# Tile 2 of x loaded on ScalarE's queue instead of SyncE's

## The chip, the cores and the metric

The kernel runs on one core of a Trainium2 chip. The metric is the device time of one execution in microseconds (us). A core has five engines with instruction streams of their own: TensorE (PE in the profile, with its weight loads PEld), VectorE (DVE), ScalarE (ACT), GpSimd (POOL) and SyncE (SP). SP, ACT and POOL also start DMA transfers; these run on the core's 16 DMA engines. A DMA started by SP stands in the profile's queue q1, one started by ACT in q10, one started by POOL in q0.

## The reference

The inputs are x (2048 tokens by 640), the attention weights wqkv (640 by 1920) and wo (640 by 640), and the weights w1 (640 by 1728) and w2 (1728 by 640) of a dense block, all in bf16. x is normalised over its 640 columns. One branch is linear attention with 32 heads of width 20, the other a two-layer block with a ReLU; the output is x + s * silu(g).

```python
xn  = layernorm(x)
q, k, v = split(xn @ wqkv)                # 32 heads, width 20
phi = lambda t: where(t > 0, t + 1, exp(t)) + 1e-6
kv  = einsum("bhsd,bhse->bhde", phi(k), v);  z = sum_s phi(k)
s   = (phi(q) @ kv / (phi(q) @ z + 1e-6)) @ wo
g   = relu(xn @ w1) @ w2
out = x + s * silu(g)
```

## The kernel before

The tokens are cut into 16 tiles of 128 rows (tile t is rows 128t to 128t+127 of x). The columns are cut into 5 chunks of 128, called k = 0 to 4, over which the products with wqkv and w1 accumulate in PSUM.

The whole kernel is a list of short words, `PROGRAM`. Each word records some operations with the tiles that they read and write. A planner (`Sched.place`, line 187) then gives every operation a time by fixed costs and puts the operations of each engine in order. PE and SP keep the order in which the words recorded them. So do all engines for the words ahead of the sign `|`; these words are called the head here. Behind the `|`, ACT, DVE and POOL take what is ready, by due time. `Sched.emit` then writes out each engine's stream with the semaphore waits. Every DMA has a semaphore of its own, and an engine that needs the data waits for it.

The planner has a model of the loads: all transfers share one line, each takes its bytes divided by a rate, and two fixed lags are added when the line passes two marks:

```python
lags = [(4.1, 0.6), (18.2, 1.2)]
...
line = max(est + (2.0 if c.turn else 1.5), line + (turned != c.turn) * (0.4 if c.turn else 0.8)) + c.byt
if lags and line > lags[0][0]:
    line += lags.pop(0)[1]
```

The words of the head that matter here:

- `lx2` loads tile 2 of x (160 KB) with SP, `ax1` loads tile 1 with ACT; both are `x_load` (line 560, the DMA at line 562).
- `lk02`, `lk24`, `lk45` load the key weights (the middle third of wqkv) in pieces of chunks 0-1, 2-3 and 4 with SP (`wk_load`, the DMA at line 586).
- `lw2`, `lw5`, `lw3`, `lw0` load pieces of w1 with SP (line 582).
- `ba0`, `bb0`, `ba3` are statistics of a tile's first or second half on DVE (`bn`, line 637). `ma0` to `ma3` are means on ACT (`mean_act`, line 685): of tiles 1 and 2 whole, of tiles 0 and 3 the second half. `sq1`, `sq2` are sums of squares on ACT (line 658).
- `ce0` to `ce3` subtract the mean on DVE (`centre`: line 699 for tiles 0 and 3, line 695 for tiles 1 and 2).
- `tr0` to `tr3` transpose a centred tile on PE (line 706), and `cd0`, `cd1`, `cd2` on DVE and `ca3` and on to `ca7` on ACT copy the transposed halves out of PSUM (lines 716 and 718): 0 and 1 are the two parts of tile 0, 2 and 3 those of tile 1, 4 and 5 those of tile 2, 6 and 7 those of tile 3.
- `k001`, `k012`, `k102` and so on are key products on PE (line 733): the first digit is the tile, the other two the range of chunks. The first two, `k001` and `k012`, need the first part of tile 0 (`cd0`) and the first key piece. `k023` is the first that needs the second piece.
- `S4`, `S5`, `S7`, `S6` are the full statistics of tiles 4 to 7 on DVE (line 637 twice and 641). `N1`, `N4`, `N5` and so on normalise a tile on DVE (line 673), and each is followed by a DMA transpose by SP (line 722), which brings the tile into the layout that the later products read. Tiles 0 to 3 thus exist twice: transposed on PE for the first key products, and transposed by DMA for what comes later.

On SP the order in the head is: loads of x tile 0, tile 2, key piece 0-1, x tile 3, key piece 2-3, x tiles 4 and 5, key piece 4, x tile 7, w1 piece 2, x tile 6, w1 pieces 5, 3 and 0, then the eight DMA transposes of tiles 1, 4, 5, 7, 6, 0, 2 and 3. ACT starts with a tiny activation (line 595), whose function table is loaded meanwhile, and the load of tile 1.

Behind the head most products use a Strassen scheme: of two tiles or blocks, sums and differences are made on DVE (line 936) and seven products on PE replace eight (line 1164 for blocks of 512 tokens, line 991 later on). The first of these sums, for the tokens 0 to 1023 (`T0`), need the DMA transposes of all the tiles 0 to 7.

Of the kernel before, what the change touches and what calls it, by code (L numbers as in the profile page):

```python
# [343 lines left out]


PROGRAM = """
lx0 lx2 ax1 ba0 mh0 ma0 lk02 lx3 lk24 ce0 lx4 ma1 ce1 lx5 lk45 lx7 lw2 tr0 pf3 cd0 lx6 bb0 ma2 sq1
ce2 cd1 ma3 tr1 k001 lw5 cd2 k012 ba3 lw3 ca3 mh3 ag0 ce3 S4 tr2 k102 S5 ca4 k023 k123 k134 ca5 k201
lw0 N1 tr3 N4 sq2 k213 S7 ca6 k035 ca7 k145 N5 ke0 k235 S6 bb3 N7 ag3 k301 k312 kr0 ke1 kr1 F1
N6 k325 ke2 P4 N0 kr2 P11 P5 F0 ke3 P10 KT5 kr3 KT4 N2 N3 |  # L350
# [1631 lines left out]
```

## Time and profile before

| what | value |
|---|---|
| median of 3 runs | 202.5 us (201.94 to 203.0) |
| profiled execution | 202.56 us |
| its span | 201.3 us |
| PE busy | 197.2 us |
| DVE busy | 173.2 us |
| ACT busy | 132.5 us |
| POOL busy | 37.7 us |
| share of the 16 DMA engines of q1, q0, q10 | 41.8%, 14.3%, 1.7% |
| granted clock of PE | 1.00 |

The span runs from the first to the last event that the profiler recorded; the execution's own time is 1.26 us longer. Rows of the timeline give the start in us from the span's start, the duration in us, the engine (with a q: its queue of DMA issues), the line, the operation, output and input, and how many instructions are merged. In brackets stands the idle time of the engine before it and what ended that. `reg` stands for several of the kernel's numbered buffers. In rows of the DMA view the last number is the median time from the start of the issue to the landing.

### The profile page before, as it was taken

To read this page: it belongs to the slowest core of one execution; us is meant where nothing else is said; L and a number is where in the kernel's file an instruction comes from. 1 tells how busy PE (TensorE), PEld (TensorE's weight loads), DVE (VectorE), ACT (ScalarE), POOL (GpSimd) and SP (SyncE) were. 2 spreads that over 40 slices of the span, in tenths; PEclk is the share of its full clock that TensorE was granted. 3 is DMA by queue.
4 is the path that set the end of the run, shared out by engine and by line. 5 is a ranking of instruction groups with operands and counts; after the bars stand their busy time and mean duration, and the time that the engine had idled before them with its cause. 6 is when DMAs were issued, how large, how long until landed. Compare 5 with 4: busy or idle time off the path is not lost.

```text
span 201.3 us, 3641 instructions
## 1 busy us (share of the span) xinstructions
PE 197.2 (98%) x1312; PEld 120.1 (60%) x1312; DVE 173.2 (86%) x407; ACT 132.5 (66%) x280; POOL 37.7 (19%) x66
## 2 busy tenths in 40 slices
PE   8899999999999999999999999999999999999995
PEld 2656534554564554545454777777777777777773
DVE  5998799999999989999568998999867699866565
ACT  6798958998999998868832514363545355536533
POOL 3584003143345646422000000000000000000000
PEclk9999999999999999999999999999999999999999
DMA  5999695345466798854304985975952711011113
GB/s 179 335 259 95 150 351 144 70 98 109 108 145 134 150 256 174 171 99 67 113 17 118 270 264 184 295 212 148 355 185 72 258 65 36 33 67 65 36 65 98
DMA packets 38455, 30.43 MB, mean 151 GB/s; under 512 B 13733, under 2 KB 38437, under 8 KB 38437
## 3 DMA queue, kind: packets, MB, share of 16 engines
q1 hardware_dynamic: 32853, 23.62, 41.8%
q0 software_dynamic: 4624, 5.57, 14.3%
q10 hardware_dynamic: 960, 1.02, 1.7%
q8 instruction: 10, 0.16, 0.4%
q14 instruction: 8, 0.07, 0.1%
HBM read 15.81 MB, written 5.24 MB: 105 GB/s over the span
## 4 chain that ended last, share of the span: by engine, by line
PE 90%; DVE 4%; DMA 2%; ACT 1%; issue 1%; DVEq 0%
PE psT L991 43%; PE psT L1164 32%; PE psT L733 6%; PE psT L1494 2%; PE psT L823 2%; DMA reg<-reg 1%; ACT regE L743 1%; PE psT L1838 1%; DMA reg<-in_A_x_dram 1%; PE psT L841 1%; PE psT L1629 1%; PE psT L1603 1%; DVE stats L637 1%; DVE regX L936 1%; PE psT L895 1%
## 5 line engine op out<-in xcount | busy, mean ns | idle before, releaser
L1164 PE MATMUL psT<-reg 128*128 128x512 bf16 (+2 forms) x166 | 45.0, 370 | 0.0
L991 PE MATMUL psT<-reg,regH 128*128 128x320 bf16 (+1 forms) x224 | 35.0, 299 | 0.0
L991 PE MATMUL psT<-reg 128*128 128x320 bf16 (+1 forms) x178 | 28.4, 299 | 0.0
L991 PEld LDWEIGHTS psT<-reg,regH 128*128 128x128 bf16 (+1 forms) x224 | 21.9, 98 | 8.5
L1164 PEld LDWEIGHTS psT<-reg 128*128 128x128 bf16 (+1 forms) x166 | 15.9, 98 | 16.9 <-DVE regH L1217 0.6
L863 POOL DMA_DIRECT2D regH<-reg x16 | 18.6, 1188 | 20.9 <-DMA regH<-reg 9.4
L991 PEld LDWEIGHTS psT<-reg 128*128 128x128 f16 (+1 forms) x178 | 17.3, 98 | 7.4 <-DVE regE L899 0.4
L936 DVE TENSOR_TENSOR reg<-reg 128x1024 f16<-128x1024 bf16 (+11 forms) x30 | 19.0, 646 | 2.2 <-PE psT L991 1.8
L998 ACT ACTIVATE reg<-psT 128x320 f32<-128x320 f32 (+1 forms) x24 | 10.5, 436 | 15.8 <-PE psT L991 14.8
L1214 ACT ACTIVATE regH<-psT 128x512 bf16<-128x512 f32 (+1 forms) x24 | 14.6, 612 | 5.8 <-PE psT L1164 5.3
L1665 ACT ACTIVATE wv_sb<-psT 128x320 bf16<-128x320 f32 (+2 forms) x23 | 9.6, 424 | 11.4 <-PE psT L991 11.0
L991 PE MATMUL psT<-reg,pqT 128*128 128x320 bf16 (+1 forms) x84 | 15.8, 299 | 0.0
L936 DVE TENSOR_TENSOR psT<-psT,reg 128x320 f32<-128x320 f32 (+1 forms) x21 | 11.4, 543 | 2.8 <-PE psT L991 2.8
L637 DVE BATCH_NORM_STATS2 stats<-reg 128x6 f32<-128x320 bf16 x28 | 12.3, 480 | 1.4 <-DMA reg<-in_A_x_dram 1.1
L1853 ACT ACTIVATE reg<-psT 128x640 bf16<-128x640 f32 (+1 forms) x14 | 8.0, 570 | 7.5 <-PE psT L991 7.5
L733 PE MATMUL psT<-reg 128*128 128x320 bf16 x80 | 12.3, 299 | 0.0
L936 DVE TENSOR_TENSOR reg<-psT,reg 128x320 bf16<-128x320 f32 (+1 forms) x16 | 7.8, 489 | 5.1 <-PE psT L991 5.1
L1171 ACT ACTIVATE psT<-psT 128x512 f32<-128x512 f32 (+1 forms) x18 | 10.6, 594 | 1.8 <-PE psT L1164 1.7
L800 ACT ACTIVATE regE<-psT 128x512 bf16<-128x512 f32 x16 | 9.5, 603 | 2.6 <-PE psT L1164 2.5
L998 ACT ACTIVATE psT<-psT 128x320 f32<-128x320 f32 x17 | 7.2, 425 | 5.6 <-PE psT L991 5.5
L936 DVE TENSOR_TENSOR reg<-reg,wv_sb 128x640 bf16<-128x640 bf16 (+1 forms) x15 | 6.8, 456 | 4.3 <-ACT reg L1853 3.5
L733 PEld LDWEIGHTS psT<-reg 128*128 128x128 bf16 x80 | 7.7, 98 | 4.5 <-issue 0.4
(174 smaller groups left out, 400.0 us busy)
## 6 DMA issues: line engine op xcount, KB each, us to landing
regH<-reg POOLq DMA_DIRECT2D x16, 320.0 KB, 3.8
reg<-in_B_w_dram SPq DMA_DIRECT2D x12, 320.0 KB, 4.9
scr<-rden SPq DMA_DIRECT2D x4, 640.0 KB, 7.0
reg<-in_A_x_dram SPq DMA_DIRECT2D x4, 640.0 KB, 6.1
out_dram<-reg SPq DMA_DIRECT2D x14, 160.0 KB, 1.8
regE<-scr SPq DMA_DIRECT2D x3, 640.0 KB, 6.1
reg<-in_A_x_dram SPq DMA_DIRECT2D x4, 320.0 KB, 4.8
reg<-in_A_x_dram SPq DMA_DIRECT2D x7, 160.0 KB, 4.3
```

Of the source, the lines that this page charges most:

```text
L637: sc.op("DVE", lambda eng: eng.bn_stats(stats[:, t, a, :], xv[:, HN * a:HN * (a + 1)]), R=[("xin", xs(t))], W=[("stats", t, a)])
L733: fns.append(lambda eng, a=a, k=k, lhs=lhs: eng.matmul(ps[bk[a]][:, 0:HN], lhsT=lhs, rhs=wk[:, k, HN * a:HN * (a + 1)], start=(k == 0), st ...
L800: exps.append(sc.op("ACT", lambda eng: eng.activation(out=e_, in_=src, func=ACTF.Exp), R=[key], W=[("er_e", es)]))
L863: dma("POOL", lambda eng: eng.dma_start(zacc[a], src, **kw), R=[key] + after, W=[("zacc", a)], chain=zchain[a])
L936: sc.op("DVE", lambda eng: eng.tensor_tensor(out=out, in0=in0, in1=in1, op=op), R=R, W=W, extra=extra)
L991: sc.group("PE", [(lambda eng, k=k, lhs=lhs, rhs=rhs: eng.matmul(ps[b][:, 0:HN], lhsT=lhs, rhs=rhs, start=(start and k == 0), stop=(k == n ...
L998: sc.op("ACT", lambda eng: eng.activation(out=dst, in_=ps[b][:, 0:HN], func=ACTF.Copy), R=[("ps", b)], W=[dkey], extra=extra)
L1164: sc.group("PE", [(lambda eng, k=k, lhs=lhs, rhs=rhs: eng.matmul(ps[b][:, 0:nn], lhsT=lhs if tile is None else rhs, rhs=rhs if tile is Non ...
L1171: sc.op("ACT", lambda eng: eng.activation(out=dst[:, 0:nn], in_=ps[b][:, 0:nn], func=ACTF.Copy), R=[("ps", b)], W=[dkey], extra=extra)
L1214: sc.op("ACT", lambda eng: eng.activation(out=dst, in_=ps[b], func=ACTF.Relu), R=[("ps", b)], W=[("hT", j, f)], extra=ex)
L1665: sc.op("ACT", lambda eng, lo=lo, hi=hi: eng.activation(out=g[:, lo:hi], in_=src[:, lo - HN * n:hi - HN * n], func=ACTF.Silu), R=[key, ("s ...
L1853: sc.op("ACT", lambda eng: eng.activation(out=o_[:, 0:n].rearrange("p (a n) -> p a n", a=2) if n == D else o_[:, 0:n], in_=src, func=ACTF. ...
```

## The change

In the first line of `PROGRAM` the word `lx2` goes, and a word `ax2` comes behind `ax1`. Tile 2 is then loaded by ACT's queue, behind tile 1, into the same buffer. SP's second transfer is the first key piece. No other word changes.

```diff
 PROGRAM = """
-lx0 lx2 ax1 ba0 mh0 ma0 lk02 lx3 lk24 ce0 lx4 ma1 ce1 lx5 lk45 lx7 lw2 tr0 pf3 cd0 lx6 bb0 ma2 sq1
+lx0 ax1 ax2 ba0 mh0 ma0 lk02 lx3 lk24 ce0 lx4 ma1 ce1 lx5 lk45 lx7 lw2 tr0 pf3 cd0 lx6 bb0 ma2 sq1
```

The word `ax` is in the table of words already: `"ax": lambda t: x_load(t, 1, "ACT")`.

## The prediction

> **What bounds the kernel now.** I read the page's busy table first, then the waits of PE, to see what its idle time is made of.
>
> ```profile
> span 201.3 us, 3641 instructions
> PE 197.2 (98%) x1312; PEld 120.1 (60%) x1312; DVE 173.2 (86%) x407; ACT 132.5 (66%) x280; POOL 37.7 (19%) x66
> ```
>
> ```profile
> PE psT L733 <- DVE regX L716: 0.6, 1, 0.6
> PE psT L1164 <- DVE psT L936: 0.2, 1, 0.2
> ```
>
> PE is busy for 197.2 of 201.3 us. Behind the warm-up it waits twice that the view lists: 0.6 us before the first key product (line 733) and 0.2 us in the first products of the blocked scheme (line 1164). So what the change can win is small, and it must pass both of these places. The next two views are the starts of the loads (the timeline; the second number is the issue's length) and, in the same order, their times from issue to landing (the DMA view, one stretch for each).
>
> ```profile
> 0.79 0.40 SPq L562 DMA_DIRECT2D reg<-in_A_x_dram  x1
> 0.96 0.39 ACTq L562 DMA_DIRECT2D reg<-in_A_x_dram  x1
> 1.25 0.42 SPq L562 DMA_DIRECT2D reg<-in_A_x_dram  x1
> 1.71 0.43 SPq L586 DMA_DIRECT2D reg<-in_A_wqkv_dram  x1
> 2.19 0.47 SPq L562 DMA_DIRECT2D reg<-in_A_x_dram  x1
> 2.70 0.47 SPq L586 DMA_DIRECT2D reg<-in_A_wqkv_dram  x1
> 3.21 0.47 SPq L562 DMA_DIRECT2D reg<-in_A_x_dram  x1
> ```
>
> ```profile
> reg<-in_A_x_dram SPq DMA_DIRECT2D x1, 160.0 KB, 2.3
> reg<-in_A_x_dram ACTq DMA_DIRECT2D x1, 160.0 KB, 2.6
> reg<-in_A_x_dram SPq DMA_DIRECT2D x1, 160.0 KB, 2.7
> reg<-in_A_wqkv_dram SPq DMA_DIRECT2D x1, 320.0 KB, 4.2
> reg<-in_A_x_dram SPq DMA_DIRECT2D x1, 160.0 KB, 4.1
> reg<-in_A_wqkv_dram SPq DMA_DIRECT2D x1, 320.0 KB, 4.5
> reg<-in_A_x_dram SPq DMA_DIRECT2D x1, 160.0 KB, 4.5
> ```
>
> Start plus landing time gives: x tile 0 at 3.1, tile 1 at 3.6, tile 2 at 3.95, key piece 0-1 at 5.9, tile 3 at 6.3, key piece 2-3 at 7.2, tile 4 at 7.7. The timeline of the three computing engines says who waits for these.
>
> ```profile
> 4.34 0.72 ACT L685 ACTIVATE regE<-reg 128x640 bf16<-128x640 bf16 x1
> 6.33 0.47 ACT L685 ACTIVATE regE<-reg 128x320 bf16<-128x320 bf16 x1 [0.46 <-DMA reg<-in_A_x_dram]
> 4.78 0.28 DVE L716 COPY regX<-psT 128x256 bf16<-128x256 bf16 x1
> 5.38 0.37 DVE L695 TENSOR_SCALAR reg<-reg,msum 128x640 bf16<-128x640 bf16 x1
> 5.67 0.55 DVE L716 COPY regX<-psT 128x384 bf16<-128x384 bf16 x2
> 6.34 0.49 DVE L637 BATCH_NORM_STATS2 stats<-reg 128x6 f32<-128x320 bf16 x1
> 7.12 0.45 DVE L699 TENSOR_SCALAR reg<-reg,msum 128x640 bf16<-128x640 bf16 x1
> 7.70 0.89 DVE L637 BATCH_NORM_STATS2 stats<-reg 128x6 f32<-128x320 bf16 x2
> 9.74 0.40 DVE L673 TENSOR_SCALAR reg<-reg,msum,rsy 128x640 bf16<-128x640 bf16 x1
> 4.97 0.44 PE L706 MATMUL psT<-ident,reg 128*128 128x128 bf16 x5
> 6.86 1.79 PE L733 MATMUL psT<-reg,regX 128*128 128x320 bf16 x12
> ```
>
> The view puts the 0.6 us wait before line 733 down to DVE's copy. But that product reads only the first copy, over at 4.78 + 0.28 = 5.06, and PE's transposes are over at 4.97 + 0.44 = 5.41. What ends at 5.9 is the key piece, so I take that load as the real releaser. On DVE, the statistics of tile 3 (6.34) and tile 4 (7.70) start where those tiles land (6.3 and 7.7); these two loads pace DVE. Behind them the first normalisation ends at 9.74 + 0.40 = 10.14. From there a second path runs beside PE:
>
> ```profile
> 6.19 3.30 SPq L582 DMA_DIRECT2D reg<-in_B_w_dram  x3
> 10.17 12.16 SPq L722 DMA_TRANSPOSE reg<-reg  x8
> ```
>
> ```profile
> 21.05 2.64 DMA reg<-reg
> ```
>
> ```profile
> 23.72 0.43 DVE L936 TENSOR_TENSOR regH<-reg 128x512 f16<-128x512 bf16 x1 [0.45 <-DMA reg<-reg]
> 27.84 0.68 DVE L936 TENSOR_TENSOR psT<-psT,wv_sb 128x512 f32<-128x512 f32 x1
> ```
>
> SP ends its loads at 9.49, waits for the first normalised tile, and issues eight transposes without a break from 10.17 to 22.33. The last one (a piece of the chain of waits) lands at 23.69, and DVE, idle 0.45 us for it, runs on to 27.84 + 0.68 = 28.52. PE's second wait ends at 28.58. So the end of the kernel hangs on this path: what PE alone wins at 6 us it waits away at 28.6.
>
> **The change, part by part.**
>
> Removed: SP's second issue (1.25, 0.42 us). Every later SP load is issued one slot earlier: the first key piece at 1.25 for 1.71 (0.46), tile 3 at 1.71 for 2.19 (0.48), tile 4 at 2.70 for 3.21 (0.51).
>
> Added: a second issue on ACT, behind the first (0.96 + 0.39 = 1.35), until about 1.74. Behind it on ACT stands the read of tile 0, which cannot begin before tile 0 lands at 3.1, so the issue costs ACT nothing. Without that cover it would cost its 0.39 us.
>
> Moved: tile 2 starts at about 1.36 for 1.25, and its packets now share the DMA engines with the key piece rather than precede it.
>
> Its landing is unknown. The lower end is the ACT queue's own row, 2.6 us: 1.36 + 2.6 = 3.96, no delay. The upper end is the price of a load served behind the key piece, as tile 3 and tile 4 are (4.1 and 4.5): 1.36 + 4.5 = 5.9. Between 2 and 3 us, where tile 0 and then tile 2 on SP's queue (q1) meet tile 1 on ACT's (q10), the DMA view of that microsecond shows:
>
> ```profile
> q1 hardware_dynamic: 133, 0.15, 48.5%
> q10 hardware_dynamic: 124, 0.15, 44.1%
> ```
>
> The two queues got nearly equal shares. With equal shares, and twice as many bytes in the key piece, tile 2 ends well before the piece; I take a landing of 4.7. The cost: ACT's mean of tile 2 moves from 4.34 to about 4.73, by 0.39. The centring that reads it (5.38) then comes between 4.73 + 0.72 = 5.45 and 5.38 + 0.39 = 5.77; I take 5.5, since DVE was busy up to 5.38. The copies behind it (5.67, 0.55 long) follow at about 5.8, and DVE reaches the statistics of tile 3 at about 6.35, as now. ACT's 0.46 us of idle time before 6.33 takes up its own delay. So at 4.7 the cost is nothing. Past about 4.9 the statistics of tile 3 begin to slip.
>
> Who gains: the key piece and all SP loads behind it. The upper end is a whole slot, 0.46 to 0.51 us, if the time from issue to landing stays. The lower end is zero: the same 800 KB (three tiles and the piece) must pass before the piece is complete. What decides between them is whether the DMA engines now have a hole that an earlier second queue can fill:
>
> ```profile
> 3.50:3.75 0.25, 0.25 (x2) 0.00 (x0) 0.21 (x2) 0.25 (x3) 0.00 (x0) 1.00 0.92 149
> 3.75:4.00 0.25, 0.25 (x2) 0.00 (x0) 0.21 (x2) 0.25 (x1) 0.00 (x0) 1.00 0.75 225
> 4.00:4.25 0.25, 0.20 (x1) 0.00 (x0) 0.25 (x2) 0.25 (x2) 0.00 (x0) 1.00 0.70 246
> 5.50:6.00 0.50, 0.00 (x0) 0.00 (x0) 0.50 (x3) 0.37 (x2) 0.04 (x1) 1.00 1.01 323
> ```
>
> In these rows by stage (last two columns: DMA share, GB/s) the engines move 149, 225 and 246 GB/s just where tile 2 ends and the key piece begins, against 323 two microseconds later. The shortfall is (174 + 98 + 77) x 0.25 / 323 = 0.27 us of transfer. I take that as the gain of the loads: key piece 5.6, tile 3 at 6.0, key piece 2-3 at 6.9, tile 4 at 7.4.
>
> PE: its first key product moves from 6.04 to about 5.75, and not before 5.41. The product k023 stands behind four of the twelve matmuls that start at 6.86 (so at about 6.86 + 4 x 1.79 / 12 = 7.4); it needs key piece 2-3, which lands at 7.2 now and keeps step.
>
> DVE and SP: the statistics of tile 4 can move from 7.70 to tile 4's new 7.4, but not before tile 3's centring of 7.12 is through. The centring of 5.38 lets DVE's next operation start 0.29 us later; this one is 0.08 us longer, so about 7.49. The gain is 0.2. The normalisation, the eight transposes, DVE's 23.72 (which has 0.45 of room) and PE's 28.58 move with it.
>
> Behind 28.6 nothing is touched, and PE has no wait that the view lists.
>
> The planned order: the planner puts transfers in one line and adds 0.6 us to the one that carries it past 4.1. By hand, its loads from tile 3 on keep their landings, tile 2 goes late in the plan, and engines move by 0.98 (DVE) to 1.01 us (PE, ACT) alike, so the order behind the head should stay. This says nothing of the chip's times; a near tie could still fall the other way.
>
> **Sum.** The profiled execution is 202.56 us (span 201.3 and 1.26 around it), 0.06 over the median of 202.5. Minus 0.2 gives 202.36, on the median's scale 202.3.
>
> **Rivals.**
>
> 1. *The transfer is hidden anyway.* The bytes ahead of the key piece stay the same, the dip just follows the first touch of the key weights to its new place, and tiles 3 and 4 land as now: 202.5. For it: 1.01 of DMA share at 5.50. Against it: the share of 0.70 to 0.75 before. The Trainium skill, page "DMA: Bandwidth & Descriptors", section "Issuing engines are not separate DMA queues", says that all issuers' transfers interleave on the same 16 engines, and that starting them from several engines saves only the issue time. By that rule, with the line to the memory full, this rival holds; the 0.70 share in this trace leaves it room to be wrong.
>
> 2. *Tile 2 too late* (the other side). It is served behind the key piece and lands at 5.9. ACT's mean then starts at 5.9 for 4.34, the centring comes about 1.3 to 1.4 later than 5.38, tile 3's statistics at about 7.5 and tile 4's at about 8.6 for 7.70: up to 0.9 slower, 203.4. It decides from a landing of about 5.0 on, where the delay at 7.70 passes zero.
>
> 3. *The order behind the head changes* on DVE, ACT or POOL by a tie. The two waits of PE are all that a better order could win (0.8); a worse one opens a wait on a PE that now has none, and one like the largest here (0.6) two or three times over gives some 204.
>
> 4. *The whole slot is won and more*: tile 3 and key piece half a microsecond earlier, tile 2 not late, and DVE saves the 0.45 before 23.72 as well: 201.9 at best by these rows.
>
> **Chances.** Forecast (0.1 to 0.35 faster) 0.43; rival 1 0.20; rival 2 0.17; rival 3 0.12; rival 4 0.08. Half a per cent is 1.0 us, about what a measurement of this kernel can tell from no change (its three runs span 201.94 to 203.0). The forecast, rivals 1 and 4 and most of rival 2 lie inside it. Slower by more: rival 3's larger part and the tail of rival 2, 0.17. Faster by more: only with a wait gone that I don't see, or a scatter of the runs, 0.09. Same: 0.74. The range takes in rival 4 with the scatter below it (201.5) and the end of rival 2 (203.4); the forecast's own is 202.0 to 202.6.
>
> **What would show it.** Right: line 733 starts at 5.6 to 5.8; the first key piece and tiles 3 and 4 land 0.2 to 0.4 earlier; tile 2 lands between 4.2 and 4.9; DVE's centring of tile 2 slips by under 0.3; the first transpose of SP stands near 9.95; DVE's wait of 23.72 and PE's wait at 28.58 are both earlier by as much. Wrong: ACT idle before tile 2's mean for over 0.7 us (rival 2); the first transpose at 10.17 with line 733 earlier (rival 1); a new row in PE's waits behind 30 us (rival 3).

## The result and the profile after

The changed kernel takes 204.09 us (median of 6 runs, 203.59 to 204.5); the kernel before took 202.68 beside it (6 runs, 201.94 to 203.0). The ratio is 1.0073, 95% interval 1.0049 to 1.0097: slower by 1.0 to 2.0 us. The prediction was 202.3, with 203.4 as its upper end. The profiled execution took 204.5 us.

The page of the changed kernel, its span and the busy time of the engines:

```profile
span 203.1 us, 3641 instructions
PE 197.4 (97%) x1312; PEld 120.2 (59%) x1312; DVE 172.7 (85%) x407; ACT 132.7 (65%) x280; POOL 37.5 (18%) x66
```

PE works as long as before (197.4 for 197.2 us), yet the span is 1.8 us longer. So PE waits, and the waits of PE in the changed kernel say where (total, times, longest):

```profile
PE psT L1164 <- DVE psT L936: 1.9, 1, 1.9
PE psT L605 <- PEq L1967: 0.8, 1, 0.8
PE psT L706 <- DVE reg L699: 0.4, 1, 0.4
PE psT L706 <- DVE reg L695: 0.3, 1, 0.3
```

The wait of 0.6 us before line 733 is gone, as the change would have it. The wait before the first products of line 1164 has grown from 0.2 to 1.9 us. Its releaser is a DVE sum into PSUM. The timeline of DVE, PE and SP around it, and the landing of the load that DVE waits for (DMA view):

```profile
23.09 0.46 SPq L567 DMA_DIRECT2D reg<-in_A_wqkv_dram  x1
27.11 0.49 DVE L761 TENSOR_TENSOR reg<-regE 128x640 bf16<-128x640 bf16 x1
29.27 0.42 DVE L936 TENSOR_TENSOR pqT<-reg 128x512 f16<-128x512 bf16 x1 [1.67 <-DMA reg<-in_A_wqkv_dram]
29.61 0.69 DVE L936 TENSOR_TENSOR psT<-psT,wv_sb 128x512 f32<-128x512 f32 x1
30.36 0.60 PE L1164 MATMUL psT<-regX,reg 128*128 128x512 f16 x2 [1.87 <-DVE psT L936]
```

```profile
reg<-in_A_wqkv_dram SPq DMA_DIRECT2D x1, 800.0 KB, 6.2
```

The same place before (the PSUM sum at 27.84 and PE's 28.58 stand in the prediction):

```profile
23.00 0.46 SPq L567 DMA_DIRECT2D reg<-in_A_wqkv_dram  x1
27.04 0.48 DVE L761 TENSOR_TENSOR reg<-regE 128x640 bf16<-128x640 bf16 x1
27.44 0.49 DVE L637 BATCH_NORM_STATS2 stats<-reg 128x6 f32<-128x320 bf16 x1
28.76 0.42 DVE L936 TENSOR_TENSOR pqT<-reg 128x512 f16<-128x512 bf16 x1
```

```profile
reg<-in_A_wqkv_dram SPq DMA_DIRECT2D x1, 800.0 KB, 5.3
```

Behind line 761 DVE now takes another operation. Before: half the statistics of x tile 8, the PSUM sum, a sum for `regX`, and only then the first sum over the query weights (`pqT<-reg`). After: the query sum first, then the PSUM sum. The query weights are loaded by SP (line 567) and land at 23.09 + 6.2 = 29.3. DVE stands before its query sum for 1.67 us, the PSUM sum stands behind it, and PE behind that. The two instruction lists differ on DVE in this place only; those of PE and POOL are the same, and SP and ACT differ by the moved load alone. DVE's, from before to after:

```
 L936 TensorTensor regE<-reg,regX 128x1024
 L761 TensorTensor reg<-regE 128x640
-L637 BNStats stats<-reg 128x6
+L936 TensorTensor pqT<-reg 128x512
 L936 TensorTensor psT<-psT,wv_sb 128x512
 L936 TensorTensor regX<-reg,pqT 128x512
-L936 TensorTensor pqT<-reg 128x512
-L637 BNStats stats<-reg 128x6
 L936 TensorTensor pqT<-pqT,reg 128x512
+L637 BNStats stats<-reg 128x6 x2
 L936 TensorTensor regH<-psT,wv_sb 128x512
```

The chain of waits of the changed kernel runs through the same place; in the chain before, from 23.72 to PE's 28.58 there was only DVE's own work, and no load.

```profile
23.09 6.16 DMA reg<-in_A_wqkv_dram
...
29.27 0.04 DVE pqT L936
...
29.61 0.70 DVE psT L936
...
30.36 4.71 PE psT L1164 x21
```

From that product to the end of the span it is 203.1 - 30.36 = 172.7 us, and 201.3 - 28.58 = 172.7 before. All of the loss is ahead of it.

At the head the change did what it says, and something more. The starts of the key piece, of tile 2 and of tile 4 (timeline), and in the same order their times to landing (DMA view), after:

```profile
1.25 0.42 SPq L586 DMA_DIRECT2D reg<-in_A_wqkv_dram  x1
1.39 0.45 ACTq L562 DMA_DIRECT2D reg<-in_A_x_dram  x1
...
2.70 0.47 SPq L562 DMA_DIRECT2D reg<-in_A_x_dram  x1
```

```profile
reg<-in_A_wqkv_dram SPq DMA_DIRECT2D x1, 320.0 KB, 3.7
reg<-in_A_x_dram ACTq DMA_DIRECT2D x1, 160.0 KB, 3.8
reg<-in_A_x_dram SPq DMA_DIRECT2D x1, 160.0 KB, 4.9
```

The key piece lands at 4.95 (5.9 before), tile 2 at 5.2 (3.95), tile 4 at 7.6 (7.7). Who waits for them (timeline after):

```profile
5.54 0.71 PE L733 MATMUL psT<-reg,regX 128*128 128x320 bf16 x4
5.26 0.74 ACT L685 ACTIVATE regE<-reg 128x640 bf16<-128x640 bf16 x1 [0.53 <-DMA reg<-in_A_x_dram]
6.12 0.39 DVE L695 TENSOR_SCALAR reg<-reg,msum 128x640 bf16<-128x640 bf16 x1 [0.36 <-ACT regE L685]
8.02 0.88 DVE L637 BATCH_NORM_STATS2 stats<-reg 128x6 f32<-128x320 bf16 x2
10.49 11.92 SPq L722 DMA_TRANSPOSE reg<-reg  x8
```

The first key product is 0.5 us earlier (6.04 to 5.54). ACT now waits 0.53 us for tile 2, the centring of tile 2 comes at 6.12 for 5.38, tile 4's statistics at 8.02 for 7.70, and the first transpose at 10.49 for 10.17.

**Why the order changed.** The planner gives DVE, when it is free, the ready operation with the earliest due time. Its own plan for the two programs (planned times; none of them is a time of the chip) reads there:

| planned, us | before | after |
|---|---|---|
| DVE is free behind line 761 | 26.231 | 27.240 |
| the query weights land | 26.254 | 27.229 |
| so DVE takes | the statistics | the query sum (due 35.95, the statistics 38.60) |

Before, the weights come 23 ns too late to be taken; after, 11 ns early enough. The plan of the changed program is shifted as a whole, since tile 2 lands late in it, but DVE's free moment by 1.009 and this load by 0.975 us. On the chip it was no tie: the weights landed 28.3 - 27.44 = 0.9 us after DVE's free moment in the run before, and 1.67 us after it in the changed one.

### The profile page after: what moved, and what is told of

The parts are those of the page before. It is cut to its first block, busy times and chain, and to the rows that moved or that the text cites. A ratio compares the mean times of both kernels' runs of the same rounds, so it can differ in the third digit from the quotient of the medians.

```text
span 203.1 us, 3641 instructions
## 1 busy us (share of the span) xinstructions
PE 197.4 (97%) x1312; PEld 120.2 (59%) x1312; DVE 172.7 (85%) x407; ACT 132.7 (65%) x280; POOL 37.5 (18%) x66
## 4 chain that ended last, share of the span: by engine, by line
PE 89%; DMA 5%; ACT 2%; DVE 1%; issue 1%; SPq 0%; DVEq 0%
PE psT L991 42%; PE psT L1164 32%; PE psT L733 6%; DMA reg<-in_A_wqkv_dram 3%; PE psT L1494 2%; PE psT L823 2%; DMA reg<-in_A_x_dram 2%; ACT regE L743 1%; PE psT L1838 1%; PE psT L841 1%; PE psT L1629 1%; PE psT L1603 1%; PE psT L895 1%; PE psT L706 0%; ACT regE L685 0%
```

## The experiments

The theory after the result: the loss is the order of DVE (theory A). The rival: it is the loads themselves, whose late tile 2 delays the transposes and with them everything behind (theory B). All edits but that of run 9 are made behind the planner in `Sched.emit`, where `recs` (or `R`) are the recorded operations by number, so that nothing else moves and the line numbers stay. From run 3 on the line `seq = self.place()` ahead of the edit is not shown again. Ratios are to the kernel before, run beside each. The expectations call run 1 e1 and run 5 e4.

**1. The new loads with the old order.** The kernel before; its tile 2 goes to ACT's queue after the planning.

```diff
-        seq = self.place()
+        seq = self.place(); self.recs[11].E = "ACT"
```

> The loads as in the changed kernel (tile 2 on ScalarE's queue, the key piece second on SyncE's), and every other engine in the order of the kernel before. Theory A (the swapped place of VectorE's first sum of the query weights is the whole loss): as before, 202.5 to 202.9 us; VectorE's wait of 1.7 us for the query weights and PE's wait of 1.9 us at the first blocked products are gone; tile 2 still lands near 5.2 us and the first transpose of SyncE stands near 10.5. Theory B (the loss comes from the loads at the head, tile 2 above all): 203.8 to 204.3 us, as the changed kernel.

Measured: 202.95 us, ratio 1.0003 (0.9981 to 1.0026), span 201.3. From its timeline:

```profile
6.45 0.39 DVE L695 TENSOR_SCALAR reg<-reg,msum 128x640 bf16<-128x640 bf16 x1 [0.87 <-ACT regE L685]
10.81 11.12 SPq L722 DMA_TRANSPOSE reg<-reg  x8
28.55 0.61 PE L1164 MATMUL psT<-regX,reg 128*128 128x512 f16 x2
```

Tile 2 is even later here (the centring at 6.45, the first transpose 0.64 later than before), and yet PE's product starts at 28.55, as before. The loads alone cost nothing that can be measured; the interval leaves room for 0.5 us.

**2. The old loads with the new order.** The changed kernel; tile 2 goes back to SP's second place after the planning.

```diff
-        seq = self.place()
+        seq = self.place(); x2 = self.recs[12]; x2.E = "SP"; seq.remove(x2); seq.insert(seq.index(self.recs[10]) + 1, x2)
```

> The loads as in the kernel before (tile 2 second on SyncE's queue), and VectorE in the order of the changed kernel. Theory A: 203.8 to 204.3 us, VectorE waits 1 to 1.7 us for the query weights just behind 27 us and PE 1 to 1.9 us at the first blocked products. Theory B: 202.5 to 202.9 us and no such wait.

Measured: 204.04 us, ratio 1.007 (1.0047 to 1.0094), span 202.6. From its timeline:

```profile
28.81 0.43 DVE L936 TENSOR_TENSOR pqT<-reg 128x512 f16<-128x512 bf16 x1 [1.43 <-DMA reg<-in_A_wqkv_dram]
29.90 0.60 PE L1164 MATMUL psT<-regX,reg 128*128 128x512 f16 x2 [1.40 <-DVE psT L936]
```

With the loads as they were, the loss is there: 1.33 us over the 202.71 beside it, 1.41 us for the whole change. Runs 1 and 2 settle it for theory A.

**3. The new order without its wait.** The changed kernel; SP issues the query weights (`wq`) ahead of x tiles 8 and 9 (`x8`).

```diff
+        x8, wq = [o for o in seq if o.kind == "dma" and o.E == "SP" and o.n >= self.head][:2]
+        seq.remove(wq); seq.insert(seq.index(x8), wq)
```

> The changed kernel, but SyncE issues the load of the query weights one place earlier, ahead of tiles 8 and 9, about 0.6 us sooner and with 320 KB less ahead of it. Theory A: the query weights land 0.7 to 1.3 us earlier, VectorE's and PE's waits shrink by as much, and the time is 202.9 to 203.5 us. Theory B: unchanged, 204.0 to 204.3 us.

Measured: 202.95 us, ratio 1.0003 (0.9974 to 1.0032). The weights land at 22.62 + 5.0 = 27.6, and neither engine waits:

```profile
27.69 0.41 DVE L936 TENSOR_TENSOR pqT<-reg 128x512 f16<-128x512 bf16 x1
...
28.77 0.60 PE L1164 MATMUL psT<-regX,reg 128*128 128x512 f16 x2
```

So it is not the order as such that costs 1.4 us, but this order with a load that is not there yet.

**4. The kernel before once more, for the head alone.**

> The kernel before once more, for a second profile: how far the landings of tile 0 (3.1 us), tile 2 (3.95), the first key piece (5.9) and tile 4 (7.7) differ between two executions of one kernel. Both theories: tile 2 near 4, the key piece near 5.9, differences of 0.3 us or less; 202.5 us.

Measured: 202.32 us (one run). The key piece landed at 1.71 + 4.0 = 5.7, tile 2 at 1.25 + 2.8 = 4.05, the first transpose was issued at 10.22, and PE's product of line 1164 started at 28.23 with no listed wait. The same program differs by 0.35 us there from one execution to another (28.58 in the other), as much as most terms of the prediction's sum.

**5. The PSUM sum first.** The kernel before; on DVE the PSUM sum (`R[231]`) goes ahead of the statistics of tile 8 (`R[167]`).

```diff
+        R = self.recs; seq.remove(R[231]); seq.insert(seq.index(R[167]), R[231])
```

> The kernel before, but VectorE makes the first PSUM sum of the blocked products (27.84 us there) ahead of the statistics of tile 8 (27.44). Theory A, extended (whatever VectorE does ahead of that sum is passed on to PE, and from there to the end): PE's wait at 28.6 us, 0.2 us as listed and 0.33 between the matmuls, is gone and the time is 0.2 to 0.35 us under the kernel before: about 202.4 us. Rival (PE is not held there, or the statistics are missed later): same or slower, 202.7 us or more.

Measured: 202.51 us, ratio 0.9978 (0.9952 to 1.0004).

```profile
27.21 0.69 DVE L936 TENSOR_TENSOR psT<-psT,wv_sb 128x512 f32<-128x512 f32 x1
...
28.29 0.59 PE L1164 MATMUL psT<-regX,reg 128*128 128x512 f16 x2
```

The sum is over at 27.9, and PE starts at 28.29 with no listed wait: 1.08 us behind its group of line 823 at 27.21, back to back. So the sum no longer holds PE. That this is a gain is not shown: 28.29 is 0.29 earlier than in one execution of the kernel before and 0.06 later than in the other (run 4), and the interval of the time touches 1.

**6. The key piece on ACT's queue instead of tile 2.** The kernel before; key piece 0-1 is ACT's second load, tile 2 stays SP's second.

```diff
+        self.recs[16].E = "ACT"
```

> The kernel before with its order, but the first key piece goes behind tile 1 on ScalarE's queue, and tile 2 stays second on SyncE's. Theory: tile 2 lands near 4.2 us, the key piece between 5.0 and 5.7, tiles 3 and 4 about 0.3 us earlier; the first transpose of SyncE comes 0.1 to 0.3 us sooner and the time is 202.4 to 202.7 us. Rival (what is won at the head is lost among the transposes): 202.7 us, with the first key product near 5.6 and no gain behind it.

Measured: 202.41 us, ratio 0.9974 (0.9943 to 1.0005).

```profile
9.95 11.91 SPq L722 DMA_TRANSPOSE reg<-reg  x8
28.10 0.61 PE L1164 MATMUL psT<-regX,reg 128*128 128x512 f16 x2 [0.17 <-DVE psT L936]
```

The key piece lands at 1.39 + 3.9 = 5.3, tile 2 at 1.25 + 2.8 = 4.05 as before, and the first key product starts at 5.44. In this execution the head has what the prediction had promised of the other edit, to the row: the first transpose at 9.95. That is luck in part: with the same loads it stands at 10.34 in run 10 and at 9.91 in run 11 (mean of the three 10.07, against 10.31 with the old loads). PE's product is at 28.10, which is 0.48 earlier than in the one execution of before and 0.13 earlier than in the other. The interval touches 1 here too.

**7. Tile 2 later still.** The kernel before; tile 2 is SP's fourth load, behind the key piece and tile 3.

```diff
+        R = self.recs; seq.remove(R[11]); seq.insert(seq.index(R[17]) + 1, R[11])
```

> The kernel before with its order, but tile 2 is SyncE's fourth transfer, behind the first key piece and tile 3: a larger dose of tile 2's delay. Tile 2 should land at 6.0 to 6.4 us. If the path from tile 2 over VectorE and the transposes to PE's wait at 28.6 is tight, the first transpose comes at 11.2 to 11.5 for 10.2 and the time is 203.3 to 203.9 us. If the stretch of the transposes takes such delays up, as e1 suggests, it is 202.7 to 203.1 us.

Measured: 203.32 us, ratio 1.0024 (0.9995 to 1.0052). Tile 2 landed at 2.23 + 3.5 = 5.7, earlier than I expected (6.0 to 6.4); the first transpose came at 10.97 and PE's product at 28.93. Against the two executions of the kernel before, the transpose is 0.80 and 0.75 later and the product 0.35 and 0.70. The median is 0.6 us over the 202.71 beside it, at the lower edge of the range for a tight path, but the interval runs from 0.1 us faster to 1.05 slower. So it excludes neither that a tile 2 this late costs nothing nor that it costs the whole delay of the first transpose.

**8. Both: the new loads and the PSUM sum first** (edits 1 and 5 on the kernel before).

> The changed loads (as e1) with VectorE's sum ahead of the statistics (as e4). If the two are independent: e1's time less e4's gain, 202.5 to 202.8 us. If tile 2's delay is what VectorE's slack pays for, the gain of e4 is lost: 202.8 us or more.

Measured: 202.49 us, ratio 0.9985 (0.9962 to 1.0008); first transpose 10.49, PE's product at 28.23 with no listed wait. The loads add nothing to edit 5 that can be measured, in either direction.

**9. The planner with a truer landing.** The changed kernel; the load of the query weights is planned 2.0 us later, and the planner orders everything behind the head anew.

```diff
-            lag = 0.5 if names[1] == "scr" else 0.8 if names[1] == "reg3" and names[0] == "reg6" else 0.0
+            lag = 0.5 if names[1] == "scr" else 0.8 if names[1] == "reg3" and names[0] == "reg6" else 2.0 if size > 8e5 and names[1] == "in_A_wqkv_dram" else 0.0
```

> The changed kernel with one number of the planner altered: the load of the query weights is planned to land 2.0 us later, about where the chip lands it. The planner orders ACT, DVE and POOL anew behind the head, in many places. Theory A (the loss comes from a plan in which this load lands too early): DVE's wait of 1.7 us for the query weights goes, and with it PE's wait of 1.9 us at line 1164: under 0.4 us each. The time is 202.4 to 203.0 if the other places of the new order are as good as the old ones, and up to 203.5 if not. Rival (the estimate matters only by the one tie, and the order found with it was good by luck): DVE's wait goes, but the new order opens another row in PE's waits behind 30 us, and the time stays at 203.8 or more.

Measured: 202.66 us, ratio 0.9996 (0.9975 to 1.0016). From its timeline:

```profile
28.01 0.60 PE L1164 MATMUL psT<-regX,reg 128*128 128x512 f16 x2
...
28.99 0.41 DVE L936 TENSOR_TENSOR pqT<-reg 128x512 f16<-128x512 bf16 x1
```

With the load planned about where it lands, the planner itself puts the query sum (28.99) behind the PSUM sum (27.27), both waits are gone, and the 1.4 us are back. It also changes other places of the order, so this run does not show that the estimate is the only thing in it that matters; that a truer estimate is enough, it does.

**10. Edits 5 and 6 together** (key piece on ACT, PSUM sum first).

> The kernel before, with key piece 0-1 loaded on ScalarE's queue behind tile 1 (tile 2 stays second on SyncE's) and with DVE's PSUM sum ahead of the statistics of tile 8. Theory A (the order of DVE behind the head sets PE's wait; the loads of the head shift the path to it by what they shift its first transpose): the two gains add, about 0.3 from the load and 0.2 from the sum: 202.0 to 202.3 beside 202.7 of the kernel before. PE starts its product of line 1164 at 27.8 to 28.1 with no wait on DVE; DVE's wait for the query weights before its first query sum grows to between 0.3 and 0.8 us, and costs PE nothing as the PSUM sum stands ahead of it. Rival (the gains are one and the same room, since PE cannot use both): 202.4 as each alone.

Measured: 202.56 us, ratio 0.9975 (0.9947 to 1.0002). The gains did not add. In the timeline of the profiled execution (202.99 us, slower than the median) a new wait follows the product:

```profile
28.06 0.59 PE L1164 MATMUL psT<-regX,reg 128*128 128x512 f16 x2
...
29.25 0.60 PE L1164 MATMUL psT<-reg 128*128 128x512 bf16 x2 [0.38 <-DMA reg<-in_A_wqkv_dram]
```

PE now waits itself for the query weights. They landed at 22.80 + 6.4 = 29.2 here; 6.4 us is the longest of all profiled executions, so the wait is in part this execution's.

**11. Edits 3, 5 and 6 together**, so that this load comes earlier as well.

> The kernel before, with key piece 0-1 on ScalarE's queue behind tile 1, DVE's PSUM sum ahead of the statistics of tile 8, and the load of the query weights ahead of that of x tiles 8 and 9 on SyncE's queue. Theory A (with the first two edits alone the query weights, landing at 29.2, are what PE waits for next, 0.4 us): the load now starts some 0.6 us earlier and lands between 27 and 28.6, neither DVE's first query sum nor PE's products of line 1164 wait over 0.2 us for it, and the time is 202.0 to 202.3 beside 202.7. Rival (the wait moves on to tiles 8 and 9, which now land later, or the end is set by something behind): 202.4 to 202.8, with a wait for these tiles on DVE or ACT that PE shows behind 30 us, or with no wait at all and the busy time of PE as the only bound.

Measured: 203.08 us (12 runs, 202.2 to 203.63), ratio 1.0013 (0.9994 to 1.0032): not better than the kernel before. Its profiled execution has PE's product at 27.76, the earliest of all, and only this wait of PE behind the first microsecond:

```profile
PE psT L1164 <- DVE regH L936: 0.2, 1, 0.2
```

But that execution took 202.27 us and was one of the two fastest of the twelve; what the slower ones do differently no profile here shows. That stays open. None of the versions beats the kernel before by more than its interval; the nearest are runs 5, 6 and 10 (ratios 0.9978, 0.9974 and 0.9975, each interval just touching 1).

The head and the product of line 1164 in all profiled executions (landings are start plus time to landing; a transpose is over when its issue on SP is; the last column is the span minus the product's start):

| run | key 0-1 lands | tile 2 lands | tile 4 lands | first 733 | first transpose | eighth transpose over | first 1164 product | span minus it |
|---|---|---|---|---|---|---|---|---|
| before | 5.9 | 3.95 | 7.7 | 6.04 | 10.17 | 22.33 | 28.58 | 172.7 |
| 4, before again | 5.7 | 4.05 | 7.8 | 5.88 | 10.22 | 21.98 | 28.23 | 172.9 |
| 2, old loads, new order | 6.2 | 4.25 | 8.0 | 6.34 | 10.47 | 22.20 | 29.90 | 172.7 |
| 5, PSUM sum first | 6.1 | 4.05 | 7.9 | 6.29 | 10.37 | 22.10 | 28.29 | 173.0 |
| after | 4.95 | 5.2 | 7.6 | 5.54 | 10.49 | 22.41 | 30.36 | 172.7 |
| 1, new loads, old order | 5.35 | 5.6 | 7.3 | 5.89 | 10.81 | 21.93 | 28.55 | 172.8 |
| 3, weights earlier | 5.65 | 5.5 | 7.8 | 5.99 | 10.69 | 22.57 | 28.77 | 172.7 |
| 8, loads and sum | 4.85 | 5.3 | 7.6 | 5.58 | 10.49 | 22.24 | 28.23 | 172.8 |
| 9, truer landing | 4.75 | 5.0 | 7.3 | 5.29 | 10.28 | 21.54 | 28.01 | 173.0 |
| 6, key piece on ACT | 5.3 | 4.05 | 7.5 | 5.44 | 9.95 | 21.86 | 28.10 | 172.8 |
| 10, key on ACT and sum | 5.7 | 4.25 | 7.9 | 5.85 | 10.34 | 22.12 | 28.06 | 173.5 |
| 11, all three | 5.0 | 4.05 | 7.4 | 5.46 | 9.91 | 21.84 | 27.76 | 173.1 |
| 7, tile 2 SP's fourth | 4.65 | 5.7 | 7.3 | 5.43 | 10.97 | 22.67 | 28.93 | 172.7 |

The first four rows have the old loads, the next five the new ones. Their means: key piece 6.0 and 5.1, tile 2 4.1 and 5.3, tile 4 7.85 and 7.5, first key product 6.14 and 5.66, first transpose 10.31 and 10.55.

## Why the prediction was wrong

**The step that failed** is "The planned order": "engines move by 0.98 (DVE) to 1.01 us (PE, ACT) alike, so the order behind the head should stay". The two numbers are nearly those of the plan, but they hold for two stretches of it. In the head DVE moves by 0.975, and SP's transposes and the load of the query weights, which stand behind them, move with it. Further on DVE waits for ACT, and at the place that counts its free moment moves by 1.009, like PE and ACT. The text did not follow the load to that place, and the conclusion was wrong: a difference of 0.03 us was called "alike", while the planner decides by which of two times comes first, however close. In the plan before, the query weights missed DVE's free moment by 23 ns; 34 ns of relative shift (1.009 - 0.975) were enough. The text had a shift of the right size and did not hold it against the nearest ties. Rival 3 named what happened, a worse order on DVE by a tie with a new wait on PE and "some 204", and got a chance of 0.12. Its size was guessed from the largest wait of before; what it really costs could have been read before the result: a query sum put ahead of the PSUM sum waits for a load that landed at 28.3, 0.9 us behind DVE's free moment, and PE with it.

**The bounds and the releaser** were right. With the old loads the first key product starts 0.13 to 0.18 us behind the landing of the key piece in all four executions, so that load was its releaser, not DVE's copy. With the new loads the piece is there 0.3 to 0.7 us ahead of it, and PE comes to the product from its transposes; that is the floor that the prediction named. The end hangs on the first products of line 1164: the last column of the table is 172.7 to 173.1 in every run but run 10, where the 0.4 us wait behind that product is in it.

**The loads' gain**, 0.3 us, was right in size for tile 4 (7.85 to 7.5 in the means), and too small for the key piece (0.9 for 0.3). That the size is right for tile 4 is luck in part. The dip that it was worked out from went on behind the three slices of the sum (287 and 266 GB/s up to 4.75), and half of the 0.27 us stood in a slice whose DMA engines were 0.92 busy, so not in a hole. With the new loads most of the dip is gone. In the windows of the changed kernel (last two columns: DMA share, GB/s) 399 GB/s stand where there were 225 before; the lower slice behind it (256) does not occur in run 1, which has 369 GB/s at 5.00:5.50 with the same loads:

```profile
3.75:4.00 0.25, 0.25 (x2) 0.00 (x0) 0.21 (x2) 0.25 (x3) 0.00 (x0) 1.00 1.08 399
5.00:5.50 0.50, 0.50 (x9) 0.43 (x10) 0.50 (x3) 0.24 (x1) 0.00 (x0) 1.00 0.94 256
```

**Tile 2's landing** was mis-sized: 4.7 foreseen between 3.96 and 5.9, 5.0 to 5.6 measured in the five executions with the new loads, 3.6 to 4.2 us from the start of its issue. The equal shares of the two queues at 2 to 3 us were the mean of two turns. In quarters of a microsecond (DMA view of before) q1 has 76.2% of the engines and q10 nothing at 2.00 to 2.25, and q1 20.6% and q10 81.1% at 2.75 to 3.00. In the changed kernel q1 has 99.0% and q10 nothing at 3.50 to 3.75, and q1 16.4% and q10 88.9% at 4.25 to 4.50. From 3.25 to 4.25 q1 moves 0.30 MB, nearly the bytes of the key piece. So tile 2 waits while the key piece has its turn, instead of sharing with it. What the key piece gained (0.9), tile 2 lost (1.2). The Trainium skill, page "DMA: Bandwidth & Descriptors", section "Issuing engines are not separate DMA queues", says that transfers from all issuers interleave on the same 16 engines, and that a second issuer saves only issue time. The traces agree with the first: the shares of q1 and q10 above add up to about the whole, and as SP's second load the key piece lands early with tile 2 on ACT's queue (4.75 to 5.65) and with both on SP's (4.65 in run 7). They do not decide on the second: on ACT's queue (runs 6, 10, 11) the key piece is issued 0.32 us earlier than with the old loads and lands 0.65 earlier by the means (5.33 for 5.98), but single landings scatter by 0.5 to 0.7.

**The first transpose** was foreseen at 9.95 and came at 10.49. Since tile 2 was past the point of about 4.9 that the text gave, rival 2's mechanism ran (ACT waits 0.53 us, the centring slips by 0.74, tile 4's statistics by 0.32), at a third of its full price.

**"The end of the kernel hangs on this path"** was right for the part behind the transposes. From the end of the eighth transpose's issue to PE's product it takes 6.25 us in both executions of the kernel before, 6.24 in run 6, 6.26 in run 7 and 6.20 in run 3; even the 0.35 us between the two executions of before is there already when that transpose is over. In run 1 it takes 6.62: there PE's matmuls stand back to back ahead of the product (its group of line 823 starts at 27.47, the product 1.08 later), so PE itself is late, while before it had 0.33 us of room at this place (27.17 to 28.58).

What is loose is the stretch of the eight transposes, called "without a break". It takes 11.70 to 11.93 us in ten of the thirteen executions, 12.16 in that of before, 11.26 in run 9 and 11.12 in run 1. Each time one of the eight takes longer to issue, in the timelines of before and of after:

```profile
17.07 2.61 SPq L722 DMA_TRANSPOSE reg<-reg  x1
```

```profile
18.46 2.62 SPq L722 DMA_TRANSPOSE reg<-reg  x1
```

Nearly all others take about 1.3 us (the last one of after: 21.13 to 22.41; the first of before took 1.59). The longest takes 2.42 to 2.64 us in eleven executions, 1.96 in run 9 and 1.82 in run 1. The stretch does not shrink for a late start (11.70 in run 7, the latest), so it does not take up a delay. That the product of run 1 came no later than before, with a first transpose 0.64 later, is in part the luck of its short stretch: with 11.70 and 6.25 it would have come at 28.76, an estimate. What shows that the loads cost little is the time of run 1 over its 12 runs, and the pairs with and without the new loads in one order (after and run 2, runs 8 and 5), which differ by 0.05 us or less.

**DVE in order.** The Trainium skill, page "PSUM — Partial Sum Buffer", section "Engine vs sequencer instructions", says that VectorE's queue is strictly first in, first out. The trace agrees: the PSUM sum started at 29.61, behind a query sum that it does not need, though in run 1, with the same loads, it could start at 27.81.

## What to carry to other kernels

Where a planner orders the work, an edit at one place is an edit at every near tie behind it: compare the instruction lists of each engine first, and if that can't be done, look for operations whose planned times lie closer than the shift that the edit makes between engines and loads. An operation that waits for a load should stand, on an engine that runs in order, behind everything that the bound engine waits for; a plan that lets a load land too early does the opposite, and with one truer estimate (run 9) the wait was gone. When two loads compete for an early place, look at who waits for which: moving the other load (runs 6, 10 and 11) brought the key piece 0.65 us forward by the means and took nothing from tile 2 (4.05 to 4.25), though none of these runs is clearly faster than the kernel before.

## What was not expected of the hardware

A 160 KB load started 0.14 us behind a 320 KB load on another queue landed 3.6 to 4.2 us after its start, against 2.7 to 3.0 us as the load ahead of it. The 320 KB load itself took 4.0 to 4.5 us in the old place and 3.5 to 4.4 in the new one.

In all thirteen profiled executions the stretch of 16 to 20 us holds one instruction fetch, here in the DMA view of before (packets, MB, share of the 16 engines):

```profile
q8 instruction: 1, 0.02, 2.4%
```

It falls where one of the eight transposes is long. In eleven executions it starts at most 0.2 us ahead of that transpose's issue, which takes 2.42 to 2.64 us, and has 2.3% to 2.7% of the engines; in runs 1 and 9 it starts about 0.4 us into the issue, which takes 1.82 and 1.96 us, and has 1.5% and 1.7%. Whether one causes the other was not tried.

The load of the query weights (800 KB, the same command in each run) took 5.3 to 6.4 us to land (5.3 before, 6.0 before again, 6.2 after, 5.9 in run 2, 6.4 in run 10), and 5.0 and 4.9 in runs 3 and 11, where it started ahead of tiles 8 and 9. With DVE waiting for it, this spread goes straight to the end: PE's wait is 1.4 us in run 2 and 1.9 in the changed kernel. In the kernel before, where the PSUM sum stands ahead of the query sum, PE does not wait for it.
